# The low part of the normed rows: a GpSimd subtraction from a float32 copy made by ScalarE, in place of one VectorE instruction

## The chip, the core and the metric

The kernel runs on one core of one Trainium2 chip. The metric is the device time of one execution in microseconds (us). A core has TensorE for matrix products (PE in the profile, with its weight loads as PEld), VectorE (DVE), ScalarE (ACT), GpSimd (POOL) and SyncE (SP), which here issues all the transfers, in order. Each engine works through its own list of instructions in order and waits on semaphores where an input comes from another engine.

## The reference

There are two stages. The first is an attention through 32 packed queries per head; batch 8, 8 heads, 576 positions, head size 64:

```
p_packed = softmax(p k^T / 8) v          # 32 rows per head
out      = softmax(q p_packed^T / 8) p_packed
```

The second takes the 4608 rows of 512 values that come out of it, `x`, and computes

```
h    = x @ w_in                          # 4608 x 1024
solu = h * softmax(h)                    # over the row of 1024
ln   = (solu - mean) / sqrt(var + 1e-06) * g_ln
y    = ln @ w_out                        # 4608 x 512
```

The results are float32. The kernel reaches the precision that they need by splitting float32 operands into a high and a low part and summing three of the four products.

## The kernel before

The packed attention and the first product are folded together: `x @ w_in` is computed as attention weights times (packed values times `w_in`), so `x` itself is never made. For each batch b, `pack(b)` makes the packed values, `unpack(b)` makes the attention weights `a2h`/`a2l` (high and low) and the folded matrix `zh`/`zl`, and both are Python generators from which the main loop takes a piece at a time between its row tiles.

The second stage goes by tiles of 128 rows, 36 in all. For each there are three functions. `mlp_in` forms `h` in PSUM (L521), takes the negated row maximum on VectorE (L523), the exponential on ScalarE (L531, into the SBUF tile `e`) and, on VectorE, `u = e * s_row * h` with the row sum `su` (L534). `mlp_norm` makes the negated mean on GpSimd (L542), writes the shifted rows in float16 into the first half of `yhl` (L544, ScalarE) and what float16 lost into the second half (L545). Both halves are turned by one transposing transfer from SP into `yT` (L547). ScalarE then squares the shifted rows, only for the sum `sq` (L549); the squares themselves go into the tile `e`, whose exponentials are no longer needed. GpSimd makes of `sq` and the sum of exponentials the row's factor `c_row` (L551 to L555). `mlp_out` multiplies `yT` with the high and low parts of `w_out` (`wch`, `wcl`), 24 matmuls of 128x512 (L564), and VectorE scales the result (L566) for the store.

`e`, `u`, `yhl` and `yT` have two buffers each. `yhl` and `yT` also hold `w_out` while it is prepared at the start (L205 to L231, L301, L321 to L330), which is why those lines show the same tile names.

The order of the row tiles on PE is: `mlp_in` of tile i, then `mlp_out` of tile i-2, with attention pieces put between and inside. From batch 1 on this order is written out by hand, for PE alone:

```
with tc.manual_schedule(engines={mybir.EngineType.PE}) if b >= 1 else nullcontext():
...
        nxt = mlp_in(row, parts)
        after()
        ready = normed.pop(0) if len(normed) > lag else None
        if summed:
            with tc.high_priority(offset=pnorm):
                normed.append(mlp_norm(*summed.pop()))
```

On ScalarE, VectorE, GpSimd and SP, and on PE in batch 0, a planner sets the order. It simulates the program with its own costs and takes, for each engine, the ready instruction of the highest priority; the `high_priority` offsets in the code shift these. So an instruction that becomes ready at another time, or runs on another engine, can change the order of everything that the planner places. After the last tile of batch 7 the loop ends with `mlp_out` of the last two tiles.

Attention instructions that share the engines: L428 and L350 (VectorE transposes of q and k), L439 (VectorE transposes of the score banks in PSUM, which PE's L467 writes two at a time), L443 to L451 (softmax, with GpSimd's L444 and L451 of 128x576), L505 to L508 (transposed weights and their two parts), L483 to L500 (the folded matrix and its two parts), L371 to L398 (exponentials and transposes of `pack`).

Of the kernel before, what the change touches and what calls it, by code (L numbers as in the profile page):

```python
# [11 lines left out]
AF = mybir.ActivationFunctionType  # L12
ALU = mybir.AluOpType
# [25 lines left out]
def packed_attention_solu_kernel(ctx: ExitStack, tc: tile.TileContext, q: bass.AP, k: bass.AP, v: bass.AP, p: bass.AP, w_in: bass.AP, w_out: bass.AP, g_ln: bass.AP, out: bass.AP):  # L39
# [13 lines left out]
    nc = tc.nc  # L53
# [483 lines left out]
    def mlp_norm(row, u, e, se, su, s_row):  # L537

        negmu = small.tile([P, 1], F32, name='negmu')
        nc.gpsimd.tensor_scalar(out=negmu, in0=su, scalar1=-1.0 / DF, scalar2=0.0, op0=ALU.mult, op1=ALU.add)  # L542
        yhl = mlp.tile([P, 2, DF], F16, name='yhl', bufs=2)
        nc.scalar.activation(yhl[:, 0], u, AF.Identity, bias=negmu)  # L544
        nc.vector.scalar_tensor_tensor(out=yhl[:, 1], in0=u, scalar=negmu, in1=yhl[:, 0], op0=ALU.add, op1=ALU.subtract)  # L545
        yT = mlp.tile([P, 2, NFC, P], F16, name='yT', bufs=2)
        nc.sync.dma_start(yT.rearrange('p t c n -> p (t c) n'), yhl.rearrange('p t f -> p (t f)'), transpose=True)  # L547
        sq = small.tile([P, 1], F32, name='sq')
        nc.scalar.activation(e, u, AF.Square, bias=negmu, accum_out=sq)  # L549
        s_eps = small.tile([P, 1], F32, name='s_eps')  # L550
        nc.gpsimd.tensor_scalar(out=s_eps, in0=se, scalar1=1e-09, scalar2=s_row, op0=ALU.add, op1=ALU.mult)  # L551
        nc.gpsimd.tensor_scalar(out=s_eps, in0=s_eps, scalar1=s_eps, scalar2=1e-06, op0=ALU.mult, op1=ALU.mult)
        c_row = small.tile([P, 1], F32, name='c_row', bufs=6)
        nc.gpsimd.tensor_scalar(out=c_row, in0=sq, scalar1=1.0 / DF, scalar2=s_eps, op0=ALU.mult, op1=ALU.add)  # L554
        nc.gpsimd.tensor_tensor(out=c_row, in0=c_row, in1=neg_half, op=ALU.pow)  # L555
        return (row, yT, c_row)
# [51 lines left out]
    def step(row, parts, knobs, work):  # L608
        lag, pout, pnorm = knobs
        before, after, mid = work  # L610
        before()
# [6 lines that stand above are left out]
        store()  # L618
        if ready:
            with tc.high_priority(offset=pout):  # L620
                mlp_out(*ready, mid)
        else:
            mid()
        summed.append(nxt)
    from contextlib import nullcontext
    for b in range(B):
        with tc.manual_schedule(engines={mybir.EngineType.PE}) if b >= 1 else nullcontext():
# [31 lines left out]
            else:  # L659
                more(12)()  # L660
    normed.append(mlp_norm(*summed.pop()))
    for tile_ in normed:
        mlp_out(*tile_)
# [26 lines left out]
```

## Time and profile before

| | |
|---|---|
| median of 3 runs | 470.95 us (470.54 to 472.06) |
| the profiled execution | 470.67 us, its span 468.9 us |
| PE busy | 430.2 us (92%) |
| VectorE busy | 354.2 us (76%) |
| ScalarE busy | 232.4 us (50%) |
| GpSimd busy | 148.0 us (32%) |
| L544 / L545 / L549, mean of one | 1149 / 1346 / 1136 ns, 36 of each |

The profile is of one execution of the program. The span runs from its first to its last instruction. A row of groups has the line, the engine, the operation, output and inputs, the count, then total and mean busy time, and the idle time of the engine just before, with what ended it. A row of the timeline begins with start and duration in us. PE's busy time is modelled from pipelined matmuls, so two of its rows can overlap.

### The profile page before, as it was taken

What the parts mean: (1) busy time and instruction counts of PE and PEld (TensorE: products, weight loads), DVE (VectorE), ACT (ScalarE), POOL (GpSimd) and SP (SyncE); (2) the same over time, 40 slices, a digit from 0 to 9 for tenths busy, and PEclk for the clock granted to TensorE, in tenths of its full rate; (3) what the DMA queues carried; (4) which work ended last, traced back from release to release, by engine and by line L of the source; (5) the groups of instructions that cost most, each with busy time, mean ns of one, the idle gap of its engine ahead of it and who ended that gap; (6) DMA issues with size and microseconds to landing.
All of it is one profiled execution on the core that took longest, in us unless ns stands there. A gap on an engine that the chain in (4) does not pass through costs nothing.

```text
span 468.9 us, 8271 instructions
## 1 busy us (share of the span) xinstructions
PE 430.2 (92%) x3116; PEld 234.7 (50%) x3116; DVE 354.2 (76%) x648; ACT 232.4 (50%) x404; POOL 148.0 (32%) x244
## 2 busy tenths in 40 slices
PE   9697795859979999999899998999999999999995
PEld 7472244633434555446544554566445555575552
DVE  3568989778768887988489979975898688655551
ACT  3577848654343653565244562653356536433430
POOL 3424556935103211421044123311342142111220
PEclk9979759988998999999999999999999999999999
DMA  9999999999569969965989588339035333526342
GB/s 265 336 268 286 152 207 124 135 193 155 110 138 185 169 127 181 191 142 95 204 111 135 109 177 154 89 69 214 23 68 113 69 69 83 119 67 134 70 101 78
DMA packets 237880, 67.00 MB, mean 143 GB/s; under 512 B 208912, under 2 KB 231440, under 8 KB 237328
## 3 DMA queue, kind: packets, MB, share of 16 engines
q1 hardware_dynamic: 237840, 66.48, 74.3%
q8 instruction: 24, 0.39, 0.4%
q14 instruction: 16, 0.13, 0.1%
HBM read 37.23 MB, written 9.44 MB: 100 GB/s over the span
## 4 chain that ended last, share of the span: by engine, by line
PE 58%; DVE 18%; DMA 10%; POOL 5%; issue 4%; SPq 2%; ACT 2%; DVEq 0%; ACTq 0%; POOLq 0%
PE po L564 30%; PE h L521 17%; DMA yT<-yhl 4%; DMA zh<-in_moe_w_in_dram 3%; PE pa L483 3%; PE pa L407 2%; PE pa L368 2%; DMA v_sb<-in_v_dram 2%; PE pa L397 2%; DVE yhl L545 2%; DVE nm L523 2%; DVE kT L350 2%; DVE u L534 1%; DMA p2raw<-in_p_dram 1%; PE pa L467 1%
## 5 line engine op out<-in xcount | busy, mean ns | idle before, releaser
L564 PE MATMUL po<-wch,yT 128*128 128x512 f16 x576 | 178.6, 380 | 4.5 <-DMA yT<-yhl 4.5
L564 PEld LDWEIGHTS <-yT 128*128 128x128 f16 x864 | 81.0, 98 | 116.5 <-issue 17.5
L564 PE MATMUL po<-wcl,yT 128*128 128x512 f16 x288 | 108.8, 379 | 0.0
L531 ACT ACTIVATE e<-h,nm 128x1024 f32<-128x1024 f32 x36 | 40.0, 1112 | 69.5 <-DVE nm L523 69.5
L521 PE MATMUL h<-zh,a2h 128*128 128x512 f32 x160 | 69.9, 437 | 1.7 <-DVE u L534 1.7
L544 ACT ACTIVATE yhl<-u,negmu 128x1024 f16<-128x1024 f32 x36 | 41.4, 1149 | 53.1 <-POOL negmu L542 51.2
L521 PE MATMUL h<-zl,a2h 128*128 128x512 f32 x160 | 64.2, 401 | 0.6 <-POOL zl L493 0.6
L521 PE MATMUL h<-zh,a2l 128*128 128x512 f32 x160 | 64.7, 404 | 0.0
L545 DVE SCALAR_TENSOR_TENSOR yhl<-u,negmu,yhl 128x1024 f16<-128x1024 f32 x36 | 48.5, 1346 | 15.5 <-ACT yhl L544 15.5
L523 DVE TENSOR_REDUCE nm<-h 128x1 f32<-128x1024 f32 x36 | 43.9, 1219 | 20.6 <-PE h L521 20.5
L534 DVE SCALAR_TENSOR_TENSOR u<-e,s_row,h 128x1024 f32<-128x1024 f32 x36 | 45.8, 1271 | 7.1 <-ACT e L531 5.0
L551 POOL TENSOR_SCALAR s_eps<-se,s_row 128x1 f32<-128x1 f32 x36 | 10.8, 301 | 110.9 <-ACT e L531 56.0
L554 POOL TENSOR_SCALAR c_row<-sq,s_eps 128x1 f32<-128x1 f32 x36 | 18.8, 521 | 78.9 <-ACT e L549 78.9
L549 ACT ACTIVATE e<-u,negmu 128x1024 f32<-128x1024 f32 x36 | 40.9, 1136 | 3.4 <-POOL negmu L542 3.4
L566 DVE SCALAR_TENSOR_TENSOR o_sb<-po,c_row,inv 128x512 f32<-128x512 f32 x36 | 26.7, 743 | 20.9 <-PE po L564 20.8
L521 PEld LDWEIGHTS h<-zh,a2h 128*128 128x128 f32 x160 | 31.2, 195 | 17.4 <-issue 8.2
L521 PEld LDWEIGHTS h<-zh,a2l 128*128 128x128 f32 x160 | 30.9, 193 | 8.7 <-DVE a2l L508 1.2
L521 PEld LDWEIGHTS h<-zl,a2h 128*128 128x128 f32 x160 | 31.0, 194 | 7.1 <-POOL zl L493 0.9
L485 ACT CAST zh<-pa 128x512 fp32r<-128x512 f32 x28 | 15.1, 583 | 23.3 <-PE pa L483 23.3
L444 POOL TENSOR_TENSOR s<-s,mx 128x576 f32<-128x576 f32 x14 | 16.9, 1229 | 30.2 <-DVE mx L443 30.1
L381 ACT ACTIVATE e<-pa,nmx 128x288 f32<-128x288 f32 x28 | 13.8, 499 | 21.6 <-DVE nmx L373 21.6
L221 POOL TENSOR_TENSOR u<-u 128x1024 fp32r<-128x1024 f32 (+1 forms) x5 | 12.9, 2573 | 28.3 <-ACT u L220 18.1
(138 smaller groups left out, 608.5 us busy)
## 6 DMA issues: line engine op xcount, KB each, us to landing
out_dram<-o_sb SPq DMA_DIRECT2D x36, 256.0 KB, 2.3
v_sb<-in_v_dram SPq DMA_DIRECT2D x16, 512.0 KB, 6.0
raw<-in_k_dram SPq DMA_DIRECT2D x28, 288.0 KB, 6.3
raw<-in_q_dram SPq DMA_DIRECT2D x96, 72.0 KB, 2.6
zh<-in_moe_w_in_dram SPq DMA_DIRECT2D x2, 1024.0 KB, 7.0
zl<-in_moe_w_in_dram SPq DMA_DIRECT2D x2, 1024.0 KB, 8.6
raw<-in_q_dram SPq DMA_DIRECT2D x4, 512.0 KB, 9.3
raw<-in_moe_w_out_dram SPq DMA_DIRECT2D x2, 1024.0 KB, 5.9
```

The source lines that it names most:

```text
L444: eng.tensor_tensor(out=s2[r], in0=s2[r], in1=mx.unsqueeze(2).broadcast_to([P, NB, J]), op=ALU.subtract)
L485: nc.scalar.copy(z_h[:, r, cols], pz)
L521: nc.tensor.matmul(h[:, 512 * n:512 * n + 512], lhsT=lhsT, rhs=z[:, r, 512 * n:512 * n + 512], start=t == 0, stop=t == len(terms) - 1)
L523: nc.vector.tensor_reduce(out=nm, in_=h, axis=AX.X, op=ALU.max, negate=True)
L531: nc.scalar.activation(e, h, AF.Exp, bias=nm, accum_out=se)
L534: nc.vector.scalar_tensor_tensor(out=u, in0=e, scalar=s_row, in1=h, op0=ALU.mult, op1=ALU.mult, accum_out=su)
L544: nc.scalar.activation(yhl[:, 0], u, AF.Identity, bias=negmu)
L545: nc.vector.scalar_tensor_tensor(out=yhl[:, 1], in0=u, scalar=negmu, in1=yhl[:, 0], op0=ALU.add, op1=ALU.subtract)
L549: nc.scalar.activation(e, u, AF.Square, bias=negmu, accum_out=sq)
L554: nc.gpsimd.tensor_scalar(out=c_row, in0=sq, scalar1=1.0 / DF, scalar2=s_eps, op0=ALU.mult, op1=ALU.add)
L564: nc.tensor.matmul(po, lhsT=yT[:, a, c], rhs=w[:, c], start=c == 0 and t == 0, stop=c == NFC - 1 and t == 2)
L566: nc.vector.scalar_tensor_tensor(out=o_sb, in0=po, scalar=c_row, in1=inv, op0=ALU.mult, op1=ALU.mult)
```

## The change

The low part was one VectorE instruction, `(u + negmu) - yhl[:, 0]`, written in float16. In its place ScalarE now makes the shifted rows a second time, in float32, into the tile `e`, and GpSimd subtracts the float16 rows from that. The tile `e` is thus written by the exponential (L531), by the copy, and by the square (L549 of before), which comes after GpSimd's reading. The transfer L547 waits for GpSimd in place of VectorE. Nothing else is changed in the program's text.

```
-        nc.vector.scalar_tensor_tensor(out=yhl[:, 1], in0=u, scalar=negmu, in1=yhl[:, 0], op0=ALU.add, op1=ALU.subtract)
+        nc.scalar.activation(e, u, AF.Identity, bias=negmu)
+        nc.gpsimd.tensor_tensor(out=yhl[:, 1], in0=e, in1=yhl[:, 0], op=ALU.subtract)
```

## The prediction

> **What bounds the kernel now.** I read the page first: engine shares, the chain that ended last and the groups.
>
> ```profile
> span 468.9 us, 8271 instructions
> PE 430.2 (92%) x3116; PEld 234.7 (50%) x3116; DVE 354.2 (76%) x648; ACT 232.4 (50%) x404; POOL 148.0 (32%) x244
> PE 58%; DVE 18%; DMA 10%; POOL 5%; issue 4%; SPq 2%; ACT 2%; DVEq 0%; ACTq 0%; POOLq 0%
> L544 ACT ACTIVATE yhl<-u,negmu 128x1024 f16<-128x1024 f32 x36 | 41.4, 1149 | 53.1 <-POOL negmu L542 51.2
> L545 DVE SCALAR_TENSOR_TENSOR yhl<-u,negmu,yhl 128x1024 f16<-128x1024 f32 x36 | 48.5, 1346 | 15.5 <-ACT yhl L544 15.5
> L549 ACT ACTIVATE e<-u,negmu 128x1024 f32<-128x1024 f32 x36 | 40.9, 1136 | 3.4 <-POOL negmu L542 3.4
> ```
>
> PE leads with 92% of the span and 58% of the chain, and VectorE follows with 76% and 18%. Shares over the whole span say nothing of a single stage, so the busy time by stage comes next.
>
> ```profile
> 70.00:100.00 30.00, 20.31 (x214) 14.11 (x213) 24.25 (x42) 20.95 (x40) 22.20 (x21) 0.93 1.07 136
> 100.00:300.00 200.00, 188.95 (x1436) 97.58 (x1437) 165.81 (x326) 95.13 (x169) 54.47 (x106) 0.97 0.88 149
> 300.00:405.00 105.00, 104.37 (x766) 57.45 (x764) 83.90 (x160) 52.98 (x92) 27.98 (x62) 1.00 0.40 90
> 405.00:458.00 53.00, 53.00 (x242) 29.76 (x242) 29.77 (x48) 20.81 (x30) 11.58 (x32) 1.00 0.44 98
> ```
>
> The columns are the stretch, then PE, PEld, DVE, ACT and POOL busy, the granted clock and DMA. From 300 to 458 us PE is busy 157.4 of 158 us, so nothing taken from VectorE can buy time there. From 100 to 300 PE has 11.05 us free, and from 70 to 100 it has 9.7 us. Those two stretches are where the change can gain. After 458 us comes the chain of the last tile, shown below.
>
> **The change part by part.** Per row tile (36 of them) VectorE loses L545 (1346 ns, 48.5 us in all). ScalarE gains a second pass over `u` with bias `negmu` and float32 output. That is the shape of L549, whose activation without its accumulator read takes 1136 ns: 36 x 1.136 = 40.9 us, ACT from 232 to 273 us, 58% of the span. GpSimd gains a two-tensor subtraction of 128x1024, float32 and float16 in, float16 out, which the trace doesn't show in that size. The nearest rows:
>
> ```profile
> L233 POOL TENSOR_TENSOR yT<-yT,u 128x1024 f32<-128x1024 f32 x1 | 2.4, 2356 | 2.8 <-DVE u L217 2.8
> L330 POOL TENSOR_TENSOR wcl<-yT,wch x3: 1155/1160/1565, 85.6 to 88.4; 128x512 f16<-128x512 f32 x3
> ```
>
> The first row is from the groups by shape. The second, from the view of the tile yT, gives minimum, median and maximum in ns: the float16 form at half the length takes 1.16 us at its median, so twice that, 2.32, is the low bound. The full length in float32 takes 2.36. A held instruction of half length took 1.57, doubled 3.1, the high bound. I take 2.35, as the float32 row has the exact length. So POOL gains 36 x 2.35 = 85 us, to 233 us or 50%.
>
> **The tail** has no cover. These are the rows of the last tile from the timelines of ACT, POOL, DVE, SP and PE:
>
> ```profile
> 452.18 1.15 ACT L544 ACTIVATE yhl<-u,negmu 128x1024 f16<-128x1024 f32 x1 [1.64 <-POOL negmu L542]
> 453.23 1.13 ACT L549 ACTIVATE e<-u,negmu 128x1024 f32<-128x1024 f32 x1
> 454.27 0.19 ACT L549 ACTIVATION_READ_ACCUMULATOR e<-u,negmu 128x1 f32 x1
> 454.62 0.73 POOL L554 TENSOR_SCALAR c_row<-sq,s_eps 128x1 f32<-128x1 f32 x1 [2.48 <-ACT e L549]
> 453.94 1.28 DVE L545 SCALAR_TENSOR_TENSOR yhl<-u,negmu,yhl 128x1024 f16<-128x1024 f32 x1
> 455.29 1.81 SPq L547 DMA_TRANSPOSE yT<-yhl  x1
> 459.60 0.39 PE L564 MATMUL po<-wch,yT 128*128 128x512 f16 x1 [1.19 <-DMA yT<-yhl]
> ```
>
> Today the subtraction ends at 453.94 + 1.28 = 455.22 and the transpose is issued 0.07 us later. PE has run out of other work and waits 1.19 us for it. After the change the float32 copy takes the slot at 453.23 and ends at 454.36. GpSimd starts about 0.16 us after ScalarE ends (454.46 to 454.62), at 454.5, and ends at 456.86. The transpose is issued at 456.93, which is 1.64 us later, and all that follows moves with it. **+1.6 us.** With the bounds of the subtraction it is +1.6 to +2.4.
>
> The square of L549 writes the same buffer `e`, so it now has to wait until GpSimd has read the copy; behind it on ScalarE stand the next tile's exponential and, with attention work about, the casts and exponentials that PE waits for. In the last stage the exponentials of the last two tiles start here:
>
> ```profile
> 441.39 1.11 ACT L531 ACTIVATE e<-h,nm 128x1024 f32<-128x1024 f32 x1 [2.82 <-DVE nm L523]
> 449.33 1.11 ACT L531 ACTIVATE e<-h,nm 128x1024 f32<-128x1024 f32 x1 [2.82 <-DVE nm L523]
> ```
>
> One tile takes 449.33 - 441.39 = 7.94 us. ScalarE in strict order would need, by the rows of the last tile above, 2.85 (449.33 to 452.18, exponential to shift), 1.05 (to 453.23), 1.13 (copy), 0.16, 2.35 (subtraction), 0.16 and 1.23 (453.23 to 454.46, square and its read): 8.93 us. It would fall behind by 1.0 us at each of the last two tiles, 2.0 us on the tail. If the planner puts the next exponential ahead of the square, it loses nothing. Both are nearly a tie (the square is ready 7.70 us after its own tile's exponential, the next exponential after 7.94), so I take about half: **+0.9**, bounds 0 and 2.0.
>
> **Between 100 and 458 us** the normed rows are ready 1.05 + 1.13 + 0.16 + 2.35 = 4.7 us after the shift starts, where nothing else holds GpSimd. In this example it is 2.98 today (158.42 - 155.44), so they come 1.7 us later:
>
> ```profile
> 155.44 1.15 ACT L544 ACTIVATE yhl<-u,negmu 128x1024 f16<-128x1024 f32 x1 [0.76 <-POOL negmu L542]
> 157.14 1.28 DVE L545 SCALAR_TENSOR_TENSOR yhl<-u,negmu,yhl 128x1024 f16<-128x1024 f32 x1
> 158.48 3.01 SPq L547 DMA_TRANSPOSE yT<-yhl  x1
> DMA to landing us min/median/max: 4.2/4.3/7.5
> 166.69 5.29 PE po L564 x24
> PE po L564 <- DMA yT<-yhl: 3.3, 3, 1.4
> ```
>
> The transpose lands at 162.8 and its matmuls start at 166.69: 3.9 us of cover, enough. PE waits for yT only 3 times from 100 to 300 us, 3.3 us in all. The longest of them is not the subtraction's doing:
>
> ```profile
> 217.62 1.28 DVE L545 SCALAR_TENSOR_TENSOR yhl<-u,negmu,yhl 128x1024 f16<-128x1024 f32 x1 [0.93 <-ACT yhl L544]
> 217.59 6.23 SPq L85 DMA_DIRECT2D raw<-in_q_dram  x9
> 227.38 3.47 SPq L547 DMA_TRANSPOSE yT<-yhl  x1
> 234.23 0.39 PE L564 MATMUL po<-wch,yT 128*128 128x512 f16 x1 [1.44 <-DMA yT<-yhl]
> ```
>
> The rows were ready at 218.90, but SP, in order, issued loads first and the transpose only at 227.38. Rows 1.7 us later still find SP busy. **0** there, as long as GpSimd isn't in the softmax when the subtraction comes. Two of its softmax instructions of 128x576, which cost about what two of 128x512 do (2.50 us at 91.07 below), would make 4.2 us of it, more than the 3.9, and PE would wait some tenths.
>
> **The first stage, 85 to 104 us,** has both signs in it:
>
> ```profile
> 91.07 2.50 POOL L322 TENSOR_TENSOR yhl<-yhl,o_sb 128x512 f32<-128x512 f32 x2
> 98.59 1.09 ACT L531 ACTIVATE e<-h,nm 128x1024 f32<-128x1024 f32 x1
> 98.79 1.28 DVE L545 SCALAR_TENSOR_TENSOR yhl<-u,negmu,yhl 128x1024 f16<-128x1024 f32 x1 [2.44 <-ACT yhl L544]
> 102.23 1.28 DVE L534 SCALAR_TENSOR_TENSOR u<-e,s_row,h 128x1024 f32<-128x1024 f32 x1
> 101.77 1.55 PE L467 MATMUL pa<-qT,ppT 64*32 64x288 f32 x16 [4.71 <-DVE s L439]
> ```
>
> VectorE stands 2.44 us before L545, which waits for ScalarE, and behind it is the transpose L439 that PE waits 4.71 us for. Without L545 in that queue up to 2.44 + 1.28 = 3.7 us of this wait can go. The matmuls behind that group need the product L534 of 102.23, whose exponential of 98.59 ended at 99.68: it could start 2.5 us earlier, and that is the most that PE can keep. Against it, GpSimd's queue is full there (22.2 of 30 us), and one subtraction placed in it before the weight products of L322 delays all behind by 2.35. Nothing in the trace says which way the planner orders that queue, so I take **0**, bounds -2.5 and +2.4.
>
> **Sum** against the profiled execution, 470.67 (span 468.9 and 1.77 around it): 1.6 + 0.9 + 0 + 0 = +2.5, 473.2. The profiled execution is 0.28 under the median of the three runs, 470.95; by the median the forecast is 473.4.
>
> [...] In the trace GpSimd's 128x1 instruction L554 takes 264 ns at its least, but it took 1.76 us from 254.91 while VectorE ran L545 and then L508:
>
> ```profile
> 254.91 1.76 POOL L554 TENSOR_SCALAR c_row<-sq,s_eps 128x1 f32<-128x1 f32 x1 [2.12 <-ACT e L549]
> L554 POOL TENSOR_SCALAR c_row<-sq,s_eps x36: 264/266/1759, 93.6 to 454.6; 128x1 f32<-128x1 f32 x36
> 255.87 0.75 DVE L508 TENSOR_TENSOR a2l<-s,a2h 128x576 fp32r<-128x576 f32 x1
> 254.76 1.19 DVE yhl L545
> ```
>
> [...]
>
> **The rivals.** (A) The square, parked behind the subtraction, holds ScalarE's queue when PE needs its casts or exponentials. For: L549 follows L544 at once in all rows above, and the buffer forces the wait. Against: ScalarE has half the span free, and the planner can put ready work ahead. A hit costs up to 0.16 + 2.35 = 2.5 us; six batches with attention beside them, one hit of half that each, 7.5 us less what cover takes, say 5: 473.4 + 5 = 478.4. (B) The other side: VectorE's queue, without an instruction that waits for ScalarE, frees the first stage. -2.5 there, and another -1, a choice, out of the 11.05 us that PE has free between 100 and 300 us, with the bare tail of +1.6: -1.9, 469.0. It decides if the 4.71 us wait before L467 falls by more than the tail adds, 1.6 us. (C) GpSimd's queue in the first stage decides: +2.4 to the forecast, 475.8. [...] (E) ScalarE never falls behind and only the bare tail is paid: 470.95 + 1.64 = 472.6; this is the near edge of the forecast and is counted with it.
>
> **How the numbers follow.** Forecast with (E) 0.45, (A) 0.17, (B) 0.23, (C) 0.10, (D) 0.05. The planner orders ScalarE, GpSimd, VectorE and SP anew, which spreads each case by a microsecond or two. The forecast's own range is 472.2 to 475. The range for 8 in 10 runs from 468.8, most of (B), to 478.5, most of (A). A measurement here can tell 0.3%, 1.4 us, from no change: under 469.5 is faster, over 472.4 slower. Faster: most of (B), 0.18. Same: the rest of (B) and the low edge of the forecast, 0.24. Slower: 0.58.
>
> **What would show it.** Right: the last transpose issued 4.7 us or more after its shift starts (3.1 today), the last PE wait near 2.8 to 4.7 us instead of 1.19, PE still without gaps from 300 to 450 us, POOL near 233 us and DVE near 306. Wrong: a GpSimd subtraction far from 2.35 us; gaps on PE released by ScalarE (A), or the wait before L467 gone and that group, now at 101.77, earlier by over 2 us (B).

## The result, and the profile after

The changed kernel takes 482.12 us (median of four runs, 480.02 to 487.05) against 470.75 (469.64 to 472.06) for the kernel before, run beside it: 1.0247 times as long, interval [1.0216, 1.0277]. The profiled execution of the changed kernel is its longest, 487.05 us; a later profile of the same program, in the last group of experiments, has 481.74. In after's profile the lines from L546 on are one higher than before's: the copy is L545, GpSimd's subtraction L546, the square L550 and the output matmul L565.

The page of after, first the engine shares and the chain that ended last, then the groups of the lines that changed:

```profile
span 485.3 us, 8281 instructions
PE 440.2 (91%) x3116; PEld 237.5 (49%) x3116; DVE 316.1 (65%) x612; ACT 270.8 (56%) x440; POOL 213.7 (44%) x280
PE 53%; DMA 9%; POOL 9%; DVE 9%; ACT 8%; SPq 5%; issue 5%; DVEq 0%; POOLq 0%; ACTq 0%
L546 POOL TENSOR_TENSOR yhl<-e,yhl 128x1024 f16<-128x1024 f32 x36 | 76.9, 2135 | 71.6 <-ACT e L545 67.9
L550 ACT ACTIVATE e<-u,negmu 128x1024 f32<-128x1024 f32 x36 | 41.3, 1147 | 49.4 <-POOL yhl L546 49.2
L545 ACT ACTIVATE e<-u,negmu 128x1024 f32<-128x1024 f32 x36 | 40.9, 1136 | 0.1
```

The copy takes 1136 ns as costed, the subtraction 2135. VectorE's busy time fell by 38 us, 10 less than the 48.5 of L545. No engine but PE is near full. What is new is in the chain and in the waits: the share of PE in the chain fell from 58% to 53% and VectorE's from 18% to 9%, ScalarE's rose from 2% to 8%, GpSimd's from 5% to 9% and SP's queue from 2% to 5%. ScalarE stands 49.2 us before its square, which waits for GpSimd. The longest kinds of PE's waits:

```profile
PE po L565 <- DMA yT<-yhl: 11.3, 6, 3.1
PE pa L397 <- ACT e L381: 6.1, 3, 3.7
```

Before, the first was 4.5 us in 4 waits, and the second 6.2 us in 3, so it is the first that grew. The busy time by stage, columns as in the prediction:

```profile
100.00:300.00 200.00, 185.45 (x1369) 94.60 (x1370) 138.13 (x287) 108.11 (x178) 80.44 (x118) 0.93 0.86 147
300.00:405.00 105.00, 102.33 (x761) 54.78 (x760) 71.26 (x146) 61.08 (x98) 47.34 (x69) 0.98 0.38 84
405.00:473.00 68.00, 66.00 (x300) 37.16 (x297) 31.14 (x59) 37.27 (x50) 29.68 (x49) 1.00 0.44 97
```

From 100 to 300 us PE is less busy (185.45 against 188.95) and its granted clock is lower (0.93 against 0.97). Between 300 and 405, where it had 0.6 us of gaps, it now has 2.7 us. So time is lost in three places: in batch 0 and just behind it, once or twice in the middle, and at the end. The third pack's transposes L397, at 133.75 us before, start 3.6 us later, and the last output group, at 459.60, starts at 474.31, 14.7 us later in this execution.

### The profile page after: what moved, and what is told of

It reads as the page before. It is cut to its first block, busy times and chain, and to the rows that moved or that the text cites. A ratio compares the mean times of both kernels' runs of the same rounds, so it can differ in the third digit from the quotient of the medians.

```text
span 485.3 us, 8281 instructions
## 1 busy us (share of the span) xinstructions
PE 440.2 (91%) x3116; PEld 237.5 (49%) x3116; DVE 316.1 (65%) x612; ACT 270.8 (56%) x440; POOL 213.7 (44%) x280
## 4 chain that ended last, share of the span: by engine, by line
PE 53%; DMA 9%; POOL 9%; DVE 9%; ACT 8%; SPq 5%; issue 5%; DVEq 0%; POOLq 0%; ACTq 0%
PE po L565 28%; PE h L521 15%; DMA yT<-yhl 6%; POOL yhl L546 4%; ACT yhl L544 2%; PE pa L483 2%; ACT e L545 2%; DVE nm L523 2%; SPq L134 2%; DMA zh<-in_moe_w_in_dram 2%; ACT e L550 2%; PE pa L407 2%; DMA raw<-in_k_dram 1%; PE pa L368 1%; ACT e L531 1%
## 5 line engine op out<-in xcount | busy, mean ns | idle before, releaser
L565 PE MATMUL po<-wch,yT 128*128 128x512 f16 x576 | 184.0, 389 | 11.3 <-DMA yT<-yhl 11.3
L565 PEld LDWEIGHTS <-yT 128*128 128x128 f16 x864 | 82.2, 99 | 128.2 <-issue 24.7
L565 PE MATMUL po<-wcl,yT 128*128 128x512 f16 x288 | 111.4, 387 | 0.0
L546 POOL TENSOR_TENSOR yhl<-e,yhl 128x1024 f16<-128x1024 f32 x36 | 76.9, 2135 | 71.6 <-ACT e L545 67.9
L521 PE MATMUL h<-zh,a2h 128*128 128x512 f32 x160 | 70.6, 442 | 1.6 <-DVE u L534 1.6
L550 ACT ACTIVATE e<-u,negmu 128x1024 f32<-128x1024 f32 x36 | 41.3, 1147 | 49.4 <-POOL yhl L546 49.2
L523 DVE TENSOR_REDUCE nm<-h 128x1 f32<-128x1024 f32 x36 | 43.9, 1219 | 37.9 <-PE h L521 37.8
L521 PE MATMUL h<-zh,a2l 128*128 128x512 f32 x160 | 65.6, 410 | 0.2 <-DVE a2l L508 0.2
L521 PE MATMUL h<-zl,a2h 128*128 128x512 f32 x160 | 65.0, 406 | 0.8 <-POOL zl L493 0.8
L531 ACT ACTIVATE e<-h,nm 128x1024 f32<-128x1024 f32 x36 | 39.7, 1104 | 20.5 <-DVE nm L523 20.5
L545 ACT ACTIVATE e<-u,negmu 128x1024 f32<-128x1024 f32 x36 | 40.9, 1136 | 0.1
L521 PEld LDWEIGHTS h<-zh,a2h 128*128 128x128 f32 x160 | 31.6, 197 | 18.2 <-issue 8.8
L521 PEld LDWEIGHTS h<-zh,a2l 128*128 128x128 f32 x160 | 31.3, 196 | 9.0 <-DVE a2l L508 1.2
L521 PEld LDWEIGHTS h<-zl,a2h 128*128 128x128 f32 x160 | 31.5, 197 | 7.1 <-POOL zl L493 1.2
L552 POOL TENSOR_SCALAR s_eps<-se,s_row 128x1 f32<-128x1 f32 x36 | 11.2, 311 | 48.6 <-ACT e L531 24.1
L555 POOL TENSOR_SCALAR c_row<-sq,s_eps 128x1 f32<-128x1 f32 x36 | 9.5, 265 | 40.2 <-ACT e L550 39.9
L485 ACT CAST zh<-pa 128x512 fp32r<-128x512 f32 x28 | 15.1, 584 | 19.2 <-PE pa L483 18.9
```

Of the source, the lines that this page charges most:

```text
L485: nc.scalar.copy(z_h[:, r, cols], pz)
L521: nc.tensor.matmul(h[:, 512 * n:512 * n + 512], lhsT=lhsT, rhs=z[:, r, 512 * n:512 * n + 512], start=t == 0, stop=t == len(terms) - 1)
L523: nc.vector.tensor_reduce(out=nm, in_=h, axis=AX.X, op=ALU.max, negate=True)
L531: nc.scalar.activation(e, h, AF.Exp, bias=nm, accum_out=se)
L545: nc.scalar.activation(e, u, AF.Identity, bias=negmu)
L546: nc.gpsimd.tensor_tensor(out=yhl[:, 1], in0=e, in1=yhl[:, 0], op=ALU.subtract)
```

## The experiments

Each kernel is built from the kernel before, so that lines are before's unless the two-line form of the change is in it. Times are medians, with the ratio to the kernel before on the same chip. In the first group four theories are named in the expectations: 1, the square held behind GpSimd's subtraction blocks ScalarE; 2, GpSimd's later and longer subtraction delays the rows; 3, ScalarE's further pass of 41 us in all; 4, the planner's new order.

**The copy written over `u`,** so that the square needs no buffer that GpSimd reads:

```
+        nc.scalar.activation(u, u, AF.Identity, bias=negmu)
+        nc.gpsimd.tensor_tensor(out=yhl[:, 1], in0=u, in1=yhl[:, 0], op=ALU.subtract)
...
-        nc.scalar.activation(e, u, AF.Square, bias=negmu, accum_out=sq)
+        nc.scalar.activation(e, u, AF.Square, accum_out=sq)
```

> ScalarE's float32 copy is written back into u in place of e, and the square reads u without a bias and writes e, so the square no longer waits for GpSimd's subtraction; ScalarE and GpSimd do the same instructions otherwise. If the held square is the main cost (theory 1): most of the loss returns, about 474 us, and ScalarE shows no wait for GpSimd's subtraction. If the later subtraction itself (GpSimd's 2.1 us behind an extra pass) is the cost (theory 2): about 480. If ScalarE's extra 41 us are the cost (theory 3): about 480. If any new order of the planner costs some us (theory 4): 476 to 480.

482.3 us, 1.0229 [1.0195, 1.0263]: nothing comes back. PE's order in batch 0 differs from after's in this kernel, so the held square alone is tested further below, with one order.

**The copy on ScalarE, the subtraction on VectorE:**

```
+        nc.scalar.activation(e, u, AF.Identity, bias=negmu)
+        nc.vector.tensor_tensor(out=yhl[:, 1], in0=e, in1=yhl[:, 0], op=ALU.subtract)
```

> The float32 copy in e stays on ScalarE, but VectorE subtracts. The square waits for VectorE. Theory 1 (the held square): the hold is as long as VectorE's 1.2 us and its queue, so about half the loss stays, 475 to 477. Theory 2 (GpSimd's duration): near 471 to 473. Theory 3 (ScalarE's extra pass): near 480. Theory 4 (order): 475 to 480.

489.33 us, 1.0381 [1.0332, 1.043], longer than after and than any of the theories had it. GpSimd isn't what the loss needs.

**GpSimd subtracts, nothing is copied** (the mean is left out of the low part):

```
+        nc.gpsimd.tensor_tensor(out=yhl[:, 1], in0=u, in1=yhl[:, 0], op=ALU.subtract)
```

> Leaves the float32 copy out: GpSimd subtracts the float16 rows from the unshifted u, so the low part lacks the mean; the instructions are otherwise those of the changed kernel. The square has no buffer to wait for and ScalarE has no extra pass. Theory 1: 471 to 473. Theory 2: GpSimd still takes 2.1 us for 1.28 but starts 1 us sooner, 475 to 479. Theory 3: 471 to 473. Theory 4: 475 to 480.

471.63 us, 1.0017 [0.9987, 1.0046]. All 36 subtractions on GpSimd cost nothing that can be measured.

**The kernel before, and a copy that nobody reads:**

```
+        nc.scalar.activation(e, u, AF.Identity, bias=negmu)
```

> The kernel before plus ScalarE's float32 copy into e, which nobody reads; VectorE makes the low part as before. The square waits for nobody. Theory 1: 471 to 473. Theory 2: 471 to 472. Theory 3 (ScalarE's extra 41 us): 478 to 482. Theory 4: 474 to 478.

482.12 us, 1.0226 [1.0209, 1.0242]. The copy alone brings a loss of the full size. That leaves theories 3 and 4, and the starts of the groups on PE tell where to look: this kernel was 9.1 us behind before at 180 us and 11.2 behind at 371; after was 6.9 behind at 180 and 12.4 at 371. Most is lost before 180 us, where PE's order is the planner's. From batch 1 on it is written by hand.

**The new path by place.** One line chooses by the tile's first row (S is 576, a batch):

```
+        (copy, GpSimd subtraction) if row >= S else (VectorE subtraction)      # "late"
+        (copy, GpSimd subtraction) if row < S else (VectorE subtraction)       # "first"
```

> The new path (copy on ScalarE, subtraction on GpSimd) only for the 31.5 tiles whose first row is 576 or later; the tiles of batch 0 keep the VectorE subtraction. TensorE's instruction order is then the one of before from end to end. Theory O (the loss is made in batch 0, where the planner with the extra pass puts two output groups ahead of an input group): 5 to 8 us of the loss go, 474 to 477 us. Theory L (ScalarE's extra 41 us delay everything in proportion): 31 of 36 copies remain, so about 10 of 11 us remain, 480 to 482. Theory K (the granted clock falls because TensorE waits more, wherever that is): between, by the waits that remain.

> The new path only for the tiles of batch 0 (4.5 of 36), the VectorE subtraction for all later ones. Theory O: 476 to 479 us, the offset of the first pack's events of batch 1 against before at +5 to +8 us by 160 us, and constant after it. Theory L: 471 to 473 us. If both this kernel and the one with the new path from batch 1 on lose some 5 us, the loss has two places.

Late: 478.69 us, 1.0152 [1.011, 1.0194]. First: 477.51 us, 1.0133 [1.0115, 1.015]. Both lose, as the last sentence of the second expectation has it. "First" is 5.8 us behind before at 180 us and 5.5 at 371; "late" is 0.6 behind at 180, 2.6 at 320 and 5.0 at 371. So neither "the order alone" nor "the load in proportion": 4.5 of 36 tiles make half the loss, and the 31.5 others the rest. PE's order, matmul by matmul, is before's in "late" and after's in "first".

**TensorE's order fixed in batch 0 too,** without and with the change:

```
-        with tc.manual_schedule(engines={mybir.EngineType.PE}) if b >= 1 else nullcontext():
+        with tc.manual_schedule(engines={mybir.EngineType.PE}) if b >= 0 else nullcontext():
```

> The kernel before, with TensorE's order in batch 0 also as written, as it is in the later batches, not by the planner: the base of a pair. It has no forecast of its own that theories differ on; some us slower than before, 472 to 485, since that order wasn't the planner's.

> The kernel after, with TensorE's order in batch 0 as written: TensorE's order is the same as in its pair partner, instruction by instruction. Theory O (order): the pair differs by 2 to 4 us (the tail and the late stages alone). Theory L (load of ScalarE): the pair differs by 10 to 13 us, as after and before do. A difference of 5 to 8 us leaves both with a part.

487.75 and 492.49 us (1.0347 [1.0327, 1.0368] and 1.0451 [1.0434, 1.0469] times before): the pair differs by 4.7 us, and until 383 us the second kernel's groups start 1.5 us earlier to 0.2 later than the first's. With one order on PE, batch 0 costs nothing; the 4.7 us come after that, with a wait of 1.94 us at L407 (385.32) and one of 3.10 for the last tile (479.51). But both kernels have three long waits in batch 0 (3.5 to 4.6 us, between 103 and 125 us), behind which a delay can hide.

**Which tiles of batch 0.** In "first", two further choices:

```
+        (copy, GpSimd subtraction) if row in [0, 256, 384, 512] else (VectorE subtraction)
+        (copy, GpSimd subtraction) if row in [128] else (VectorE subtraction)
```

> The new path for four of batch 0's five tiles (all but the one at row 128), VectorE's subtraction elsewhere. The planner then puts the fourth tile's input group earlier than before, not behind two output groups. Theory O (what batch 0 loses is TensorE's order): at most 2 us of the 6 that all five tiles cost, 471 to 473.5. Theory L (ScalarE's extra passes in batch 0): four fifths of 6, 475.5 to 477.

> The new path for the tile at row 128 alone, VectorE's subtraction for the 35 others. The planner then moves an input group 20 rows further back, behind two output groups, as in the kernel that copies for nobody. Theory O: 4 to 8 us slower than before, 475 to 479, with a wait of TensorE for the exponentials of the third pack of over 2 us. Theory L: one fifth of 6, 472 to 473.

Four tiles: 471.7 us, 1.0007 [0.9988, 1.0026], no loss. One tile: 478.56 us, 1.0152 [1.013, 1.0174], more than all five together. Four passes of ScalarE in batch 0 are free. What the costly one goes with is another place of the input group of the fifth tile (row 512; the expectations count from nought and call it the fourth). Six of its 24 matmuls come early; the others stand behind 38 output matmuls (L564) in before, behind 48 with the one tile, 46 in after and in "first", and 64 with the copy alone. In the two kernels that lose nothing it is 27 (four tiles) and 38 (GpSimd subtracts, nothing is copied). The count isn't all: with the copy over `u` it is 34, and that kernel loses time, with a wait of 4.06 us for transposed rows at 109.48. No run has the order of the one-tile kernel without its pass, so the two aren't parted entirely; the pass is 1.1 us of ScalarE and 2.1 of GpSimd, the loss 7.5 us. Timeline rows of before, PE and VectorE:

```profile
118.58 0.50 PE L521 MATMUL h<-zh,a2h 128*128 128x512 f32 x1
122.02 1.05 DVE L371 TENSOR_REDUCE mx<-pa 128x1 f32<-128x288 f32 x2
125.73 1.22 DVE L523 TENSOR_REDUCE nm<-h 128x1 f32<-128x1024 f32 x1 [1.11 <-PE h L521]
133.75 1.59 PE L397 MATMUL pa<-ident,e 128*128 128x128 f32 x8 [1.03 <-ACT e L381]
```

The same steps with the one tile, and then in after:

```profile
119.67 0.58 PE L521 MATMUL h<-zh,a2h 128*128 128x512 f32 x1
124.80 0.82 DVE L371 TENSOR_REDUCE mx<-pa 128x1 f32<-128x288 f32 x2 [3.99 <-PE pa L368]
128.37 1.22 DVE L523 TENSOR_REDUCE nm<-h 128x1 f32<-128x1024 f32 x1 [1.20 <-PE h L521]
137.05 2.71 PE L397 MATMUL pa<-ident,e 128*128 128x128 f32 x10 [4.71 <-ACT e L381]
```

```profile
122.82 0.58 PE L521 MATMUL h<-zh,a2h 128*128 128x512 f32 x1
129.43 1.23 DVE L523 TENSOR_REDUCE nm<-h 128x1 f32<-128x1024 f32 x1 [0.91 <-PE h L521]
137.39 1.58 PE L397 MATMUL pa<-ident,e 128*128 128x128 f32 x8 [2.05 <-ACT e L381]
```

Output matmuls of finished tiles now stand on PE ahead of the scores (L368) and the input group (L521) on which a chain of VectorE and ScalarE hangs: row maximum, exponential, product, shift, and the third pack's exponentials. The chain starts 2.6 us (one tile) and 3.7 us (after) later by L523, and PE, out of output work by then, waits 4.71 and 2.05 us for it in place of 1.03.

**A wait paid twice?** Behind the long waits the granted clock fell. Windows of "first" behind its 2.19 us wait at 108.33 and from 138 to 152 us, and the second window of before (columns: stretch, PE busy, clock, DMA):

```profile
108.30:112.30 4.00, 3.97 (x11) 0.59 1.05 187
138.00:152.00 14.00, 10.93 (x137) 0.53 0.89 177
```

```profile
138.00:152.00 14.00, 11.94 (x92) 0.88 0.93 172
```

The first window loses 4 x 0.41 = 1.6 us, but that is no loss against before, which has a clock of 0.50 from 101.26 to 108.09, behind its 4.71 us wait. L397 starts 136.45 - 133.75 = 2.7 us later, 1.0 of it by the longer wait. From there to the next pack's scores L368 "first" needs 163.19 - 136.45 = 26.74 us, before 156.96 - 133.75 = 23.21, so 3.5 us more are lost. Together these are 6.2, about the 6.0 that "first" costs. By the clock records of the traces PE is at 0.50 for 20.48 us between 90 and 163 us in "first" and for 10.24 in before, so up to 5.1 us of it can be the clock's. To test the clock's part, matmuls of ones were put in, in "first" ahead of L397 and in "late" between the last two output groups:

```
+  pt = ps_a.tile(...); [matmul(pt, lhsT=ones, rhs=ones...) for _ in range(8 if b == 2 and i0 == 0 else 0)]
+  ... [matmul(hx[:, :512], lhsT=ones, rhs=ones...) for _ in range(12)] if tile_ is normed[-1] else None
```

> The kernel with the new path in batch 0 only, and 8 matmuls of ones into the tile that the transposes of the third pack's first group then overwrite, so that TensorE works in the 2.05 us in which it waits for ScalarE's exponentials there; every other instruction of TensorE stands as in its partner (477.5 us). Theory C (the idle stretch brings the granted clock to 0.50 for the 11 us from 138.5 us on, and that is most of what batch 0 loses): the clock stays near 1.00 there and 2.5 to 4.5 us come back, 473 to 475. Theory O alone (the order of the groups costs the time, the clock goes its own way): 477 to 479.

> The kernel with the new path from batch 1 on, and 12 matmuls of ones between the last two output groups, where TensorE waits 3.08 us for the last transposed tile and runs at 0.50 to 0.67 for 4 us behind it. Theory C: the last group runs at full clock, the stretch from its start to the end is 1 to 2 us shorter, 477 to 478 (478.7 without). Otherwise: the same end, or up to 0.5 us later if the fill outlasts the wait.

In "first" the time is the same, 477.43 us, 1.0119 [1.0069, 1.0169]:

```profile
137.21 2.12 PE L391 MATMUL pa<-ones 128*128 128x512 f32 x8 [2.05 <-ACT e L381]
138.00:152.00 14.00, 11.41 (x160) 1.00 0.88 176
```

The fill itself waited the 2.05 us, as its bank is one that the exponentials read, so it came behind the wait and added 2 us of work. The clock rose from 0.53 to 1.00, and 2 us more work fitted into the same time; more isn't shown here. Two things stand beside this. The wait of 2.05 us is still there and the clock didn't fall behind it; in "first" a second wait, of 0.75 us at 138.79, follows, and here the fill leaves 0.20 us of it. And L368, at 162.40, has a new wait of 1.83 us for VectorE's L500, with 0.50 for 3.4 us behind it, which takes up part of what was won. In "late" it sits right. Its tail, without and with the fill:

```profile
466.95 0.61 PE L564 MATMUL po<-wch,yT 128*128 128x512 f16 x1 [3.08 <-DMA yT<-yhl]
466.90:470.00 3.10, 3.05 (x8) 0.50 0.01 3
```

```profile
461.93 3.08 PE L663 MATMUL h<-ones 128*128 128x512 f32 x12
465.37 0.39 PE L564 MATMUL po<-wch,yT 128*128 128x512 f16 x1 [0.36 <-DMA yT<-yhl]
465.30:468.40 3.10, 3.03 (x14) 1.00 0.01 4
```

From the start of the first to that of the last matmul of the last group it is 6.60 us without and 4.98 with the fill (before: 4.97). So the wait of 3.08 us at this tail cost 1.6 us more behind it, and work without meaning took that away. The whole kernel, 477.54 us, 1.0146 [1.01, 1.0191], is 1.2 us shorter in its median, within the intervals. In "late" the clock is 0.50 for 3.41 us from 466.86, and 1.00 before and after it.

**The held square, and the last batch.** "Late" once with the copy written over `u`, and once without the last batch (`S <= row < 7 * S`):

> The new path from batch 1 on with the copy written over the shifted rows themselves and the square read from there, so that the square no longer waits for GpSimd; TensorE's order is that of its partner (478.7 us). Theory H (the held square delays what stands behind it on ScalarE, seen as the 1.93 us wait for the transposed exponentials at 372.8 us and part of the last tile's 3.08): these go to under 0.5 and near 2.5 us, and 2 to 4 us come back. Theory P (the pass itself): nothing comes back, 478 to 479.

> The new path for the tiles of batches 1 to 6 only: neither batch 0 nor the last batch has it. Against the kernel with it from batch 1 on (478.7 us) this takes away the last tile's longer chain. Theory T (the tail is worth its longer wait of 1.9 us and the clock behind it): 474.5 to 476. If the whole loss lay in the middle: 478; if it all lay in the last batch: 471 to 472.

In place: 477.06 us, 1.0116 [1.007, 1.0162], 1.6 less than "late" in the medians, not told apart by the intervals. Its wait at 372.77 is gone, but four others of 0.63 us for the transposed exponentials came. Middle only: 475.61 us, 1.0095 [1.006, 1.013]. So batches 1 to 6 cost 4.3 us, and the last batch 478.69 - 475.61 = 3.1 (by the two ratios 2.7). PE's order is before's in both. In the middle the rows of this kernel show two hits. ScalarE, GpSimd and PE of this kernel at the first of them:

```profile
369.12 1.05 ACT L398 COPY e1T<-pa 128x512 f32<-128x512 f32 x2
369.29 2.14 POOL L545 TENSOR_TENSOR yhl<-e,yhl 128x1024 f16<-128x1024 f32 x1 [2.31 <-ACT e L545]
371.47 1.15 ACT L549 ACTIVATE e<-u,negmu 128x1024 f32<-128x1024 f32 x1 [1.30 <-POOL yhl L545]
372.62 0.35 ACT L398 COPY e1T<-pa 64x256 f32<-64x256 f32 x1
373.02 1.15 PE L407 MATMUL pa<-v_sb,e1T 64*32 64x64 f32 x48 [1.94 <-ACT e1T L398]
```

The square stands between two pieces of L398, waits for GpSimd, and the second piece, for which PE waits, comes behind both. This wait of 1.9 us is in every kernel whose square is held behind GpSimd from batch 1 on, and in none of the others. The other hit is a transposed tile, the 17th. Before, then middle only:

```profile
271.35 1.28 DVE L545 SCALAR_TENSOR_TENSOR yhl<-u,negmu,yhl 128x1024 f16<-128x1024 f32 x1 [0.84 <-ACT yhl L544]
280.52 3.58 SPq L547 DMA_TRANSPOSE yT<-yhl  x1
287.59 0.39 PE L564 MATMUL po<-wch,yT 128*128 128x512 f16 x1 [1.10 <-DMA yT<-yhl]
```

```profile
272.97 2.14 POOL L545 TENSOR_TENSOR yhl<-e,yhl 128x1024 f16<-128x1024 f32 x1 [2.69 <-ACT e L545]
282.15 5.01 SPq L547 DMA_TRANSPOSE yT<-yhl  x1
289.26 0.39 PE L564 MATMUL po<-wch,yT 128*128 128x512 f16 x1 [2.23 <-DMA yT<-yhl]
289.20:293.20 4.00, 3.94 (x11) 0.58 0.74 140
```

The rows of this tile were ready at 272.63 and are now at 275.11, each time 7 us or more before SP issues their transpose, since SP works through loads until then (to 280.4 and 282.1). So it is SP's queue that sets this wait, and not the subtraction of this tile. SP's loads start 0.5 us later than before (268.28 against 267.78), in a kernel that runs 0.5 us late there, behind the transpose of the tile before, which waited for GpSimd until 266.17 (263.16 for VectorE in before); the rest of the 1.6 us came within the loads, and why isn't shown. PE's wait grows by 1.1 us, and 4 x 0.42 = 1.7 go to the clock behind it. But the same wait is 1.35 us in "first" and with the four tiles, 1.77 with the one tile and 1.92 in the filled kernel below, which have no pass here at all. That the change lengthens it isn't settled.

**The kernel before, filled,** in the 4.71 us wait at 101.77, with 56 small score matmuls into an unused bank:

> The kernel before with 56 further small matmuls (2.5 us at full clock) into an unused bank around the second score group of batch 1's unpack, where TensorE waits 4.71 us and then has a granted clock of 0.50 for 6 us. Theory C (the idle stretch lowers the clock): clock near 1.00 at 102 to 108 us, 1 to 3 us faster than before, 468 to 470. Against it: the fill lets the planner order batch 0 otherwise (an input group earlier), which may cost or gain 3 us.

473.37 us, 1.0058 [1.0027, 1.0089]. The clock is 1.00 from 102 to 150 us as theory C has it, but the kernel is slower: the fill changed the planner's order, and its third pack's values are 3.3 us late. What the clock is worth in time it can't say, and as a repair it fails.

**The change once more,** beside these three:

> The kernel after, once more, beside the three above on one chip. All theories: 480 to 484. What is compared is its parts: batch 0 alone cost 6.0, batches 1 to 6 alone 4.3, and the last batch on top 3.1; if they add, the sum is 13.4 and this is 484.5; if the late waits overlap with what batch 0 has already delayed, 480 to 482.

482.18 us, 1.0239 [1.0196, 1.0282]. The parts, 6.0 + 4.3 + 3.1, make 13.4; the whole is 11.1. They overlap by some 2 us, about what their intervals allow; it isn't settled which.

**The passes without the places:**

```
+        (copy over u from batch 1 on, GpSimd subtraction) if row < 7 * S and row != 128 else (VectorE subtraction)
+        square of u without bias where u is overwritten
```

> The new path for 31 of 36 tiles: not for the tile at row 128, which moved TensorE's order, and not for the last batch's four; in batches 1 to 6 the copy is written over the shifted rows and the square read from there, so that it waits for nothing. TensorE's order is that of the four-tile kernel (471.7 us). Theory O+T (order, held square and tail are the whole loss; ScalarE's 35 us of further passes as such cost nothing): 471 to 474. Theory L (the passes cost in proportion): 31 of 36 of the 11 us, 480 to 481. From the parts: 471.7, and of the in-place kernel's 5.8 us what isn't its tail (a wait 1.4 longer and 1.4 of slower matmuls), 3.0: 474.7.

475.11 us, 1.0077 [1.006, 1.0093]. The sum of the parts (474.7) held; "471 to 474" was a microsecond short. So the 31 passes still cost 3.5 us. At the score groups of 185.98 and 379.21 this kernel is 1.4 and 3.6 us behind before, so some 2 us of it are lost in between. Two of PE's waits show where:

```profile
PE pa L407 <- ACT e1T L398: 2.5, 4, 0.6
PE pa L368 <- DVE zl L500: 2.1, 2, 1.1
```

Neither is among the waits of before. Both hang on attention pieces (L398, and L485 ahead of L500) that share ScalarE with the passes. No version tried is faster than the kernel before.

## Why the prediction was wrong

The sign was right; the forecast of 473.4 us was 8.7 short of 482.12, and that is outside the range of 468.8 to 478.5. By its steps:

**The instructions:** the copy was right to the nanosecond (1.136 us). The subtraction took 2.13 us where 2.35 was taken, under its low bound of 2.32, which had been doubled from half-length rows.

**The tail, +1.6, and ScalarE behind, +0.9,** were right as mechanisms, and the term that was left out is the clock. After, the rows of DVE, ACT, POOL, SP and PE for the last tile:

```profile
460.49 1.23 DVE L523 TENSOR_REDUCE nm<-h 128x1 f32<-128x1024 f32 x1 [1.94 <-PE h L521]
461.57 1.15 ACT L550 ACTIVATE e<-u,negmu 128x1024 f32<-128x1024 f32 x1 [2.25 <-POOL yhl L546]
462.72 1.09 ACT L531 ACTIVATE e<-h,nm 128x1024 f32<-128x1024 f32 x1
465.54 1.15 ACT L544 ACTIVATE yhl<-u,negmu 128x1024 f16<-128x1024 f32 x1 [1.63 <-POOL negmu L542]
467.81 2.13 POOL L546 TENSOR_TENSOR yhl<-e,yhl 128x1024 f16<-128x1024 f32 x1 [2.30 <-ACT e L545]
469.96 1.80 SPq L548 DMA_TRANSPOSE yT<-yhl  x1
474.31 0.39 PE L565 MATMUL po<-wch,yT 128*128 128x512 f16 x1 [3.09 <-DMA yT<-yhl]
```

From shift to transpose it is 469.96 - 465.54 = 4.42 us against 3.11, so the chain grew by 1.3. The exponential of 462.72 had its row maximum at 461.72 and stood 1.0 us behind the square, where before it waited for VectorE. The order was the strict one, for which the sum had 2.0 us, but ScalarE needed 8.41 us per tile (454.31 to 462.72) and not 8.93, so it fell behind by 0.5 us at each of the last two tiles. That the +0.9, taken as half of the 2.0, is near the 1.0 that came is luck. PE's wait grew by 1.9 us. Then the last group ran 1.7 us longer (6.66 against 4.97), at a clock of 0.50 for 3.41 us; the filled tail of "late" shows that to be the wait's doing. The sum had no term for what a wait costs behind itself. The last batch measured 3.1 where 2.5 stood.

**"Between 100 and 458 us: 0"** failed: 4.3 us in batches 1 to 6, and PE isn't without gaps from 300 to 450 us. The step looked at the transposed rows alone. Its reading that SP's loads, and not the subtraction, come last there holds for the wait at 287.59 too. What it left at nothing is ScalarE's queue with the attention pieces in it: rival (A), at a chance of 0.17 and a price of 5 us, came once in this stage. Its mechanism was right; the hit was 1.9 us, and 1.7 more where the clock fell behind it (in after 0.50 for 3.41 us from 379.31; behind the same wait, 1.94 us in middle only and 1.93 in the second profile of after, it stayed at 1.00). Without the held square the further passes still cost some 2 us in this stage (the last kernel above). How the 4.3 us divide between these isn't fully shown.

**"The first stage: 0, bounds -2.5 and +2.4"** failed most: 6.0 us, outside of both bounds. Rival (B)'s relief did come: in after the score group behind the long wait starts at 98.69, not 101.77, which is the sign that had been named for (B). PE kept none of it, since the first output group then waits 2.68 us for rows that are ready at 94.14 and whose transpose SP issues at 104.60, behind four loads (99.38 in before). The four-tile kernel has such a wait too, 2.53 us at 109.28, and loses nothing, so the 6.0 us aren't this wait's. Rows of PE and SP:

```profile
98.69 1.25 PE L467 MATMUL pa<-qT,ppT 64*32 64x288 f32 x16 [1.30 <-DVE s L439]
100.01 4.49 SPq L85 DMA_DIRECT2D raw<-in_q_dram  x4
104.60 2.32 SPq L548 DMA_TRANSPOSE yT<-yhl  x1
109.18 0.39 PE L565 MATMUL po<-wch,yT 128*128 128x512 f16 x1 [2.68 <-DMA yT<-yhl]
```

The cause, as far as the runs show it, is the planner's new order of TensorE's own groups, and it was in none of the cases: (C) had the queue of GpSimd, and the last section of the working let the planner spread each case by "a microsecond or two". The one-tile kernel shows 7.5 us from one tile's pass.

**(D), at a chance of 0.05.** No run shows its term, a loss of some us on PE from a VectorE that stands behind GpSimd's subtractions; that was the author's estimate. In after PE waits for VectorE's L508 once, for 0.2 us. L508 itself takes 2.23 us at 357.83, where it takes 0.72 at 356.02, while GpSimd's subtraction runs:

```profile
357.83 2.23 DVE L508 TENSOR_TENSOR a2l<-s,a2h 128x576 fp32r<-128x576 f32 x1 [0.42 <-ACT a2h L507]
357.32 2.13 POOL L546 TENSOR_TENSOR yhl<-e,yhl 128x1024 f16<-128x1024 f32 x1 [1.95 <-ACT e L545]
```

GpSimd's subtraction ends at 359.45, and L508 0.61 us later. Each of the five L508 of after that start during a subtraction (at 207.01, 262.62, 305.81, 357.83 and 401.45 us) ends 0.61 or 0.62 us behind it. Over the span L508 takes 18.1 us in place of 11.6, so VectorE paid 6.5. L554 on GpSimd (L555 in after) fell from 521 ns to 265 in the mean; in before, its 1.76 us from 254.91 end 0.05 us behind VectorE's L508 (255.87 and 0.75 us). The kernel in which GpSimd subtracts and nothing is copied loses nothing that can be measured (471.63 us, 1.0017).

## What to carry to other kernels

Where a planner sets an engine's order, an added instruction on another engine can move whole groups of the engine that bounds the kernel, so bound that step by the length of a group and the chain behind it, not by the length of the new instruction; and try the change with one order on the bounding engine, or tile by tile, before blaming the instruction. For a kernel that TensorE bounds, look for each wait that already exists on a chain that you lengthen: it has no cover (the last tile's grew from 1.19 to 3.09 us). And before you call a wait covered or not, find out whether the chain or another queue sets it. Count a long wait of TensorE twice, once as itself and once as the slower matmuls behind it: 3.09 us at the tail of after had 1.7 us more behind it. With the waits of 1.9 to 2.3 us here that happened in some and not in others (next section).

## What the runs showed of the hardware

The granted clock of TensorE after an idle stretch was not expected in this size. In the clock records of before and after it is 1.00 or 0.50 and nothing between. From 90 us to the last matmul every stretch at 0.50 lasts 3.41 us or a multiple of that: 6.83 and 3.41 in before, and in after 6.83, 3.41, 13.65 and three times 3.41. The 0.53 to 0.59 of the windows above are means of the two levels.

Away from other waits, those of 1.0 to 1.5 us left it at 1.00: 1.03 us at 133.75, 1.44 at 234.23, 1.10 at 287.59 and 1.19 at 459.60 in before, 1.20 at 197.73 in after. From 1.9 to 2.3 us it went both ways. In after 1.88 us at 296.53 left it, and 2.20 at 241.80 had 0.50 for 3.41 us from 242.78 behind it; in the second profile of after 2.27 us at 292.86 left it. In middle only 2.00 us at 235.48 left it, and 2.23 at 289.26 had the 0.58 of the window above behind it. The same wait of 1.93 us at L407 left it in the second profile of after (374.88) and had 0.50 for 3.41 us behind it in the first (378.52); what decides isn't shown. At 2.5 us and more it fell in each of these: with 4.71 us in before (0.50 from 101.26), with 2.68 and 3.09 in after (from 109.66 and 474.88), with 3.08 in "late" (from 466.86). Behind three short waits of 0.6 to 0.7 us within 5 us it was at 0.50 from 142.22 to 145.64 in the kernel before, and at 1.00 behind three such waits (141.75, 143.78 and 145.47) in the filled one.

From 90 us to the last matmul the clock is at 0.50 for 10.24 us in before and for 23.89 in the second profile of after. That is at most 5.1 and 11.9 us of lost time, so 6.8 of the 11.1 us by which the two spans differ (468.9 and 479.9). It is no proof that the clock is the cause of so much: in batch 0 the fill raised it and only 2 us came back.
